# Attention and mixture of experts on one core: x kept as two fp16 halves from the attention on, and x^T made by transposing these halves

## The chip, the cores and the metric

The kernel runs on one core of one Trainium2 chip. The core has five engines that run side by side, each through its own list of instructions in order: PE (TensorE, matrix products and transposes), DVE (VectorE), ACT (ScalarE), POOL (GpSimd) and SP (SyncE, which here only issues transfers). An engine that has to wait for another holds everything behind it in its own list. The metric is the device time of one execution in microseconds (us); for several executions the median is given.

## The reference

All arithmetic is in fp32. Shapes: q, k, v (8, 8, 576, 64), w_gate (512, 8), w1 (8, 512, 1024), w2 (8, 1024, 512).

```python
out_up = repeat(softmax_attention(mean4(q), mean4(k), mean4(v)), 4)   # on 144 positions
out_local = softmax_attention(q, k, v, only where |i - j| < 4)
x = (out_up + out_local) as [4608 tokens, 512]
logits = x @ w_gate
# the 36864 logits from the largest down: a token goes to the expert of its largest
# logit whose capacity of 576 tokens is not used up
for e in range(8):
    out[tokens of e] = maximum(x[tokens of e] @ w1[e], 0) @ w2[e]
```

`softmax_attention` subtracts the row maximum, takes the exponent, divides by the sum and multiplies with v; the scores have the factor 1/8.

## The kernel before

**Halves.** Where an fp32 value enters a product on PE, it is split into two fp16 numbers: hi is the value times a scale, rounded, and lo is what is left. A product of two such values is three fp16 products: hi hi, hi lo, lo hi. ACT makes each hi, DVE each lo (value times scale minus hi).

**Attention (up to about 296 us).** The tokens are worked in 36 units of 128, four and a half to a batch. The order of every engine's instructions is written out: a table `LOC` gives each step of a unit u a lag, and the steps of all units are issued in the order of u + lag, with the loads and the downsampled attention of each batch (queries and keys averaged over four, tiles kdt, qdz, sd, ptd) placed between them. For one unit: `s0`, `s1` (lag 0.33) compute the local scores on PE; DVE takes the maximum (mx, L444) and subtracts it (sw, L445); ACT takes the exponent of sw (L446), which is issued three steps later; `t` (1.3) transposes sw on PE (L454), and ACT copies it to pt (L465); `v0`, `v1` (1.83) multiply with v on PE (L476), and DVE divides by the sum into the tile x (L404 to L407). `up` (1.7) loads the downsampled result of the unit's rows from DRAM through SP (L416), and `add` (4.5, L484) adds it to x, on DVE for the units under 28 and on POOL from there. `st` (4.6, L487) stores x as fp32 to DRAM from SP. `lt` (5.61, L494 to L499) transposes x on PE as four 128x128 fp32 blocks, ACT makes the hi half of x^T out of PSUM and DVE the lo half two steps later; `lm` (8.07, L509 to L514) multiplies these with w_gate into the logits lg. The tile x has 6 buffers, xt 3; all PSUM tiles of the attention are one tile `g` with 8 buffers.

**Routing.** The greedy assignment is a chain of short steps on DVE, PE and ACT (comparisons cmp, counts pR, cs, fl), one pass for each expert. It ends in the list idx of an expert's tokens. The pass for the first expert stands alone (296 to about 334 us); the pass for expert i + 1 runs beside the products of expert i.

**Experts (334 to 787 us).** Here the order comes from a scheduler with priorities. `gather` fetches the 576 rows of x for an expert in five blocks (four of 128 tokens, one of 64) by indirect transfers from POOL into xg (L1061, 5 buffers). They become x^T, tile xt, in one of two ways. For expert 0, `piece` transposes the four fp32 128x128 parts of a block on PE into a PSUM tile pX (L1070), and ACT and DVE split them (L1073, L1074). For experts 1 to 7, `piece_dma` splits the rows first, on ACT and DVE into the tile xs (L1080, L1081, 2 buffers), and SP then issues a transfer that transposes both halves (L1082). `mlp` multiplies with w1 into pH (L1097), ACT and DVE split relu(pH) into ht (L1110, L1113), and the second product goes tile by tile into pX (L1126): tiles c0 to c3 of 128 tokens and c4 of 64. ACT scales a tile into y (L1131), and POOL scatters it to the output (L1134). pX has 2 buffers. The table `GET` places the transposing of expert i + 1: its blocks 0 and 1 after tile c0 of expert i, blocks 2 and 3 after c1, block 4 after c2. The weights are loaded as nat and split into wh and wl (L1044, L1046).

Of the kernel before, what the change touches and what calls it, by code (L numbers as in the profile page):

```python
# [43 lines left out]
FL = 3  # L44
FT = 2
# [4 lines left out]
LOC = {'up': 1.7, 'st': 4.6, 't': 1.3, 'lm': 8.07, 's0': 0.33, 's1': 0.331, 'lt': 5.61, 'v0': 1.83, 'v1': 1.831, 'add': 4.5}  # L50
GS1 = ''
# [4 lines left out]
UB = 3  # L56
XB = 6
NPT = 2
# [18 lines left out]
EN0 = 24  # L77
TB = 3
SUM0 = (0.55, 1.4, 1.89)
# [10 lines left out]
class Attention:  # L90
    def __init__(self, ctx, tc, q, k, v, wg, ident, identb, maskc, x_dram, up_dram, lg, big, more=()):
# [13 lines left out]
        self.load_nat(0, "t")  # L105
        self.ident, ident = ident
        identh = cst.tile([128, 130 + H], BF, name="identb")
# [25 lines left out]
    def gate(self):  # L133
        nc = self.nc
        nc.scalar.activation(self.wg16[:, :, 0], self.wgf, AF.Copy, scale=GS)
        nc.vector.scalar_tensor_tensor(self.wg16[:, :, 1], self.wgf, GS, self.wg16[:, :, 0],
                                       op0=OP.mult, op1=OP.subtract)
# [343 lines left out]
    def log_a(self, u):  # L481
        nc = self.nc
        x = self.x[u]
        (nc.gpsimd if u >= ADDU else nc.vector).tensor_tensor(x, x, self.up[u], op=OP.add)  # L484

    def store(self, u):
        getattr(self.nc, STQ).dma_start(self.x_dram[128 * u:128 * u + 128], self.x[u])  # L487

    def log_t(self, u):
        nc = self.nc  # L490
        x = self.x[u]
        p = self.ps.tile([128, 4, 128], F32, name="g", bufs=8)
        for c in range(4):
            nc.tensor.transpose(p[:, c], x[:, 128 * c:128 * c + 128], self.ident)  # L494
        xt = self.wk.tile([128, 2, 4, 128], F16, name="xt", bufs=TB)
        pf = p.rearrange("p c t -> p (c t)")
        hi = xt[:, 0].rearrange("p c t -> p (c t)")
        nc.scalar.activation(hi, pf, AF.Copy, scale=XS)
        self.after(FT, lambda: nc.vector.scalar_tensor_tensor(xt[:, 1].rearrange("p c t -> p (c t)"), pf, XS, hi,  # L499
                                                              op0=OP.mult, op1=OP.subtract), ("x", u))  # L500
        self.xt[u] = xt

    def log_m(self, u):
        nc = self.nc
        self.need(("x", u))
# [32 lines left out]
    def run(self, after, ready):  # L538
        self.so, self.x, self.up, self.xt, self.ptd = {}, {}, {}, {}, {}
        self.warm()  # L540
# [12 lines left out]
        for b in range(B):  # L553
# [28 lines left out]
            "st": lambda u: lambda: self.store(u),  # L582
            "add": lambda u: lambda: self.log_a(u),
            "lt": lambda u: lambda: self.log_t(u),
            "lm": lambda u: lambda: self.log_m(u),
# [33 lines left out]

W1S, W2S, XM = 64.0, 64.0, 8.0  # L620
LOP = 512
# [3 lines left out]
HALF = {16: ((0, NT),), 32: ((0, 20), (20, NT)), 64: ((0, 20), (20, NT)), 128: ((0, 12), (12, 24), (24, NT))}  # L625
XSB = 2
LOE = "vector"
RACT = True
# [16 lines left out]
class Routing:  # L645
# [37 lines left out]
    def open(self, ctx, ps, ident):  # L683
# [6 lines left out]
        self.t128 = wk.tile([128, NT, 18], BF, name="t128")  # L690
        self.id16 = wk.tile([128, 128], F16, name="id16")
        nc.scalar.copy(self.id16, ident)
        nc.scalar.dma_start(self.tri, consts["tri"])
# [307 lines left out]
class Experts:  # L1001
# [50 lines left out]
    def gather(self, idx, first):  # L1052
# [5 lines left out]
        for c, (s0, n) in enumerate(SL):  # L1058
            xg = self.wk.tile([128, HD], F32, name="xg", bufs=5)
            with self.tc.high_priority():  # L1060
                self.fetched = nc.gpsimd.indirect_dma_start(out=xg[:n], out_offset=None, in_=self.x,  # L1061
                                                            in_offset=bass.IndirectOffsetOnAxis(
                                                                ap=idx[:n, c:c + 1], axis=0))
            xgs.append(xg)

        def piece(c):
            s0, n = SL[c]
            p = self.ps.tile([128, 4, 128], F32, name="pX", bufs=2)
            for d in range(4):
                nc.tensor.transpose(p[:, d, :n], xgs[c][:n, 128 * d:128 * d + 128], self.ident[:n, :n])  # L1070
            hi, lo = xt[:, 0, :, s0:s0 + n], xt[:, 1, :, s0:s0 + n]
            with self.tc.high_priority():
                nc.scalar.activation(hi, p[:, :, :n], AF.Copy, scale=XM)  # L1073
                nc.vector.scalar_tensor_tensor(lo, p[:, :, :n], XM, hi, op0=OP.mult, op1=OP.subtract)  # L1074

        def piece_dma(c):
            s0, n = SL[c]
            xs = self.wk.tile([128, 2, HD], F16, name="xs", bufs=XSB)
            with self.tc.high_priority():
                nc.scalar.activation(xs[:n, 0], xgs[c][:n], AF.Copy, scale=XM)  # L1080
                getattr(nc, LOE).scalar_tensor_tensor(xs[:n, 1], xgs[c][:n], XM, xs[:n, 0], op0=OP.mult, op1=OP.subtract)  # L1081
                nc.sync.dma_start_transpose(xt[:, :, :, s0:s0 + n].rearrange("p a d s -> p (a d) s"),  # L1082
                                            xs[:n].rearrange("p a d -> p (a d)"))

# [64 lines left out]
def moe_attention(tc, q, k, v, wg, w1, w2, cst, out):  # L1149
    nc = tc.nc  # L1150
    with ExitStack() as top:
        dr = top.enter_context(tc.tile_pool(name="dr", bufs=1, space=DRAM))
        keep = top.enter_context(tc.tile_pool(name="keep", bufs=1))
        x_dram = dr.tile([NTOK, HD], F32, name="x_dram")
        up_dram = dr.tile([B * G, HD], F32, name="up_dram")
        lg = keep.tile([128, NT, E], F32, name="lg")
        ident = keep.tile([128, 128], F32, name="ident")
        ro = Routing(top, tc, lg, cst)
        big = top.enter_context(tc.tile_pool(name="big", bufs=6))
        with ExitStack() as ctx:  # L1160
            with tc.manual_schedule(engines=ORD):
                at = Attention(ctx, tc, q, k, v, wg, (ident, cst["ident"]), cst["identb"], cst["mask"], x_dram, up_dram,
                               lg, big, ((ro.tabs, cst["tabs"]),))
                at.run(lambda a, b: ro.setup(a, b, True), ro.ready)
        with ExitStack() as ctx:
            ps = ctx.enter_context(tc.tile_pool(name="mps", bufs=1, space=PSUM))
            ro.open(ctx, ps, ident)
            ex = Experts(ctx, tc, x_dram, w1, w2, out, ident, ps, big)
            with tc.high_priority(TOP):
# [98 lines left out]
```

## Time and profile before

| | us |
|---|---|
| three runs, median | 799.38 |
| lowest and highest of them | 798.59, 804.76 |
| the profiled execution | 796.83 |
| its span in the profile | 795.0 |
| busy in the span: PE, DVE, ACT, POOL | 684.7, 562.3, 333.4, 235.1 |

The granted clock of TensorE was 0.928 of full speed on the mean. A line of a group reads: source line, engine, operation, output <- input (partitions x elements, type), count | busy us, mean ns of one | us for which the engine sat idle just before such an instruction, and what it waited for. A line of the timeline reads: start us, us, engine, line, operation, tiles, count, and in brackets the idle time before it with what ended it; an entry with xN holds N instructions. SPq is the queue of transfers that SP issues. A line of waits reads: waiter <- what ended the wait: us in all, times, longest.

### The profile page before, as it was taken

To read this page: it belongs to the slowest core of one execution; us is meant where nothing else is said; L and a number is where in the kernel's file an instruction comes from. 1 tells how busy PE (TensorE), PEld (TensorE's weight loads), DVE (VectorE), ACT (ScalarE), POOL (GpSimd) and SP (SyncE) were. 2 spreads that over 40 slices of the span, in tenths; PEclk is the share of its full clock that TensorE was granted. 3 is DMA by queue.
4 is the path that set the end of the run, shared out by engine and by line. 5 is a ranking of instruction groups with operands and counts; after the bars stand their busy time and mean duration, and the time that the engine had idled before them with its cause. 6 is when DMAs were issued, how large, how long until landed. Compare 5 with 4: busy or idle time off the path is not lost.

```text
span 795.0 us, 21152 instructions
## 1 busy us (share of the span) xinstructions
PE 684.7 (86%) x8545; PEld 472.8 (59%) x8545; DVE 562.3 (71%) x1679; ACT 333.4 (42%) x631; POOL 235.1 (30%) x274
## 2 busy tenths in 40 slices
PE   6687988796988873499889899999999979999994
PEld 4576877685877752365456356456456456574752
DVE  6878877977797887887869889888869335172210
ACT  3456756573767440342525234234324134252210
POOL 9264463735355440300400412130220311301001
PEclk8789998998999995599989999999999999999997
DMA  9949979697999850611825744480946832704001
GB/s 265 210 129 238 244 195 268 183 255 204 254 228 211 201 173 9 207 66 59 274 60 212 139 151 162 85 307 2 245 147 233 177 113 94 166 1 100 21 28 34
DMA packets 152901, 126.18 MB, mean 159 GB/s; under 512 B 96996, under 2 KB 127204, under 8 KB 152804
## 3 DMA queue, kind: packets, MB, share of 16 engines
q1 hardware_dynamic: 145424, 103.30, 49.9%
q0 software_dynamic: 6432, 20.98, 8.7%
q8 instruction: 68, 1.11, 0.6%
q10 hardware_dynamic: 948, 0.55, 0.3%
q14 instruction: 29, 0.24, 0.1%
HBM read 95.30 MB, written 21.23 MB: 147 GB/s over the span
## 4 chain that ended last, share of the span: by engine, by line
issue 30%; PE 25%; DVE 20%; DMA 13%; ACT 5%; POOL 4%; SPq 2%; POOLq 0%; ACTq 0%; DVEq 0%
PE pH L1097 7%; PE pX L1126 3%; DMA xt<-xs 3%; POOL out_dram L1134 3%; DMA nat<-in_v_dram 2%; DVE cmp L700 2%; PE g L476 2%; PE g L436 2%; PE g L292 2%; DMA xg<-x_dram,idx 2%; PE pR L726 1%; DMA up_dram<-xu 1%; DVE x L407 1%; PE g L454 1%; PE g L325 1%
## 5 line engine op out<-in xcount | busy, mean ns | idle before, releaser
L1097 PE MATMUL pH<-xt,wh 128*128 128x256 f16 (+1 forms) x1024 | 200.1, 291 | 5.7 <-DMA xt<-xs 5.0
L1126 PE MATMUL pX<-wh,ht 128*128 128x512 f16 (+1 forms) x640 | 183.3, 384 | 0.2 <-ACT y L1131 0.2
L1097 PE MATMUL pH<-xt,wl 128*128 128x320 f16 (+1 forms) x512 | 148.5, 290 | 0.0
L1126 PEld LDWEIGHTS <-ht 128*128 128x128 f16 (+1 forms) x960 | 81.5, 101 | 89.2 <-issue 6.4
L1134 POOL DMA_INDIRECT out_dram<-y,idx x40 | 41.2, 1031 | 289.5 <-ACT y L1131 262.9
L1126 PE MATMUL pX<-wl,ht 128*128 128x512 f16 (+1 forms) x320 | 119.3, 384 | 0.0
L1097 PEld LDWEIGHTS <-wh 128*128 128x128 f16 x1024 | 98.2, 99 | 33.2 <-issue 9.1
L1110 ACT ACTIVATE ht<-pH 128x512 f16<-128x512 f32 (+1 forms) x128 | 45.5, 407 | 128.3 <-PE pH L1097 128.3
L1046 DVE SCALAR_TENSOR_TENSOR wl<-nat,wh 128x512 f16<-128x512 f32 x128 | 85.2, 682 | 2.5
L1113 DVE SCALAR_TENSOR_TENSOR ht<-pH,ht 128x512 f16<-128x512 f32 (+1 forms) x128 | 52.4, 450 | 38.7 <-ACT ht L1110 38.3
L1061 POOL DMA_INDIRECT xg<-x_dram,idx x40 | 43.3, 1083 | 118.2 <-DVE idx L997 57.1
L1131 ACT ACTIVATE y<-pX 128x512 f32<-128x512 f32 (+1 forms) x40 | 23.6, 593 | 117.7 <-PE pX L1126 76.4
L1044 ACT ACTIVATE wh<-nat 128x1024 f16<-128x1024 f32 x64 | 66.8, 1055 | 6.6 <-DMA nat<-in_moe_w_dram 6.5
L1081 DVE SCALAR_TENSOR_TENSOR xs<-xg,xs 128x512 f16<-128x512 f32 (+1 forms) x35 | 23.5, 687 | 50.3 <-ACT xs L1080 50.1
L1097 PEld LDWEIGHTS <-wl 128*128 128x128 f16 x512 | 50.6, 99 | 13.0 <-issue 0.4
L465 ACT COPY pt<-g 64x512 f32<-64x512 f32 x72 | 41.8, 580 | 34.2 <-PE g L454 33.0
L292 PE MATMUL g<-ident,nat 128*128 128x128 f32 x256 | 41.7, 292 | 13.7 <-DMA nat<-in_q_dram 9.5
L476 PE MATMUL g<-vw,pt 128*64 128x65 f32 x1152 | 44.5, 230 | 2.4 <-DMA up_dram<-xu 1.4
L476 PEld LDWEIGHTS g<-vw,pt 128*64 128x64 f32 x1152 | 39.5, 143 | 8.4 <-ACT pt L465 4.5
L278 ACT COPY kt<-g 64x512 f32<-64x512 f32 (+1 forms) x56 | 35.1, 627 | 20.7 <-PE g L292 13.8
L278 ACT COPY qz<-g 64x512 f32<-64x512 f32 (+1 forms) x52 | 33.0, 634 | 21.4 <-PE g L292 19.1
L265 POOL TENSOR_TENSOR gtmp<-qz 64x576 f32<-64x576 f32 x28 | 32.5, 1160 | 30.7 <-DVE kdt L268 29.1
(219 smaller groups left out, 1180.1 us busy)
## 6 DMA issues: line engine op xcount, KB each, us to landing
nat<-in_moe_w_dram SPq DMA_DIRECT2D x28, 1024.0 KB
vw<-in_v_dram SPq DMA_DIRECT2D x136, 96.0 KB
up<-up_dram SPq DMA_DIRECT2D x36, 256.0 KB
x_dram<-x SPq DMA_DIRECT2D x36, 256.0 KB
nat<-in_q_dram SPq DMA_DIRECT2D x16, 512.0 KB
nat<-in_k_dram SPq DMA_DIRECT2D x16, 512.0 KB
nat<-in_v_dram SPq DMA_DIRECT2D x14, 512.0 KB
up_dram<-xu SPq DMA_DIRECT2D x16, 128.0 KB
```

Source lines behind the costliest of these rows:

```text
L278: self.nc.scalar.copy(out, in_)
L292: nc.tensor.transpose(p[:, a, :, fp], src[:, 4 * hh + 2 * a + s, 2 * fp:2 * fp + 2].rearrange("p f d -> p (f d)"), self.ident)
L465: self.nc.scalar.copy(out, in_)
L476: nc.tensor.matmul(o[64 * i:64 * i + 64, 65 * h:65 * h + 65], pt[:, 2 * g + i, h].rearrange("p b q -> p (b q)"), self.vw[u % 4][:, i, 4 * ...
L1044: nc.scalar.activation(hi, r, AF.Copy, scale=sc)
L1046: nc.vector.scalar_tensor_tensor(lo[:, a:a + LOP], r[:, a:a + LOP], sc, hi[:, a:a + LOP], op0=OP.mult, op1=OP.subtract)
L1061: self.fetched = nc.gpsimd.indirect_dma_start(out=xg[:n], out_offset=None, in_=self.x, in_offset=bass.IndirectOffsetOnAxis(ap=idx[:n, c:c ...
L1097: mm = nc.tensor.matmul(p[:, s, :s1 - s0], w[d][a][:, 128 * f:128 * f + 128], xt[:, b, d, s0:s1], start=j == 0, stop=j == len(seq) - 1)
L1110: last = nc.scalar.activation(hi, q, AF.Relu)
L1113: nc.vector.scalar_tensor_tensor(lo, q, 0.0, hi, op0=OP.max, op1=OP.subtract)
L1126: nc.tensor.matmul(p[o:o + m], ht[:, f, h0:h0 + m], w[4 + f // 2][b][:, 512 * (f % 2):512 * (f % 2) + 512], start=j < parts, stop=j >= len ...
L1134: i = nc.gpsimd.indirect_dma_start(out=self.out, in_=y[:n], in_offset=None, out_offset=bass.IndirectOffsetOnAxis(ap=idx[:n, c:c + 1], axis=0))
```

## The change

x leaves the attention as two fp16 halves. Two new steps follow the add: `hi` (lag 4.6) makes 32 x rounded to fp16 on ACT, out of the SBUF tile x, and `lo` (4.85) the rest on DVE; both go into a new tile xh with 2 buffers. `st` (now 4.9) stores xh, so that a row of x in DRAM is 1024 fp16 numbers in place of 512 fp32 ones. `lt` transposes the halves as eight fp16 blocks into one PSUM tile, and ACT copies all 1024 columns at once; the DVE step behind it is gone, and `lm` comes a unit earlier (7.07). `gather` fetches the halves. Experts 0 and 1 (`ROWS = 2`) now have their blocks transposed on PE, eight fp16 parts each, with a copy on ACT and one on DVE; experts 2 to 7 have them transposed by the transfer straight out of xg, and the tile xs with its two operations is gone. x's scale XM goes from 8 to 32, xg from 5 to 7 buffers, x from 6 to 4, xt of the attention from 3 to 2, and the fp16 identity is made during the attention.

```diff
-LOC = {'up': 1.7, 'st': 4.6, 't': 1.3, 'lm': 8.07, ..., 'lt': 5.61, 'v0': 1.83, 'v1': 1.831, 'add': 4.5}
+LOC = {'up': 1.7, 'hi': 4.6, 'lo': 4.85, 'st': 4.9, 't': 1.3, 'lm': 7.07, ..., 'lt': 5.61, 'v0': 1.83, 'v1': 1.831, 'add': 4.5}
-XB = 6
+XB = 4
+XHB = 2
-TB = 3
+TB = 2
+    def high(self, u):
+        nc = self.nc
+        self.xh[u] = self.wk.tile([128, 2, HD], F16, name="xh", bufs=XHB)
+        nc.scalar.activation(self.xh[u][:, 0], self.x[u], AF.Copy, scale=XS)
+
+    def low(self, u):
+        nc = self.nc
+        xh = self.xh[u]
+        nc.vector.scalar_tensor_tensor(xh[:, 1], self.x.pop(u), XS, xh[:, 0], op0=OP.mult, op1=OP.subtract)
+
     def store(self, u):
-        getattr(self.nc, STQ).dma_start(self.x_dram[128 * u:128 * u + 128], self.x[u])
+        getattr(self.nc, STQ).dma_start(self.x_dram[128 * u:128 * u + 128], self.xh[u].rearrange("p a d -> p (a d)"))
     def log_t(self, u):
-        p = self.ps.tile([128, 4, 128], F32, name="g", bufs=8)
-        for c in range(4):
-            nc.tensor.transpose(p[:, c], x[:, 128 * c:128 * c + 128], self.ident)
+        p = self.ps.tile([128, 2, 4, 128], F16, name="g", bufs=8)
+        for a in range(2):
+            for c in range(4):
+                nc.tensor.transpose(p[:, a, c], xh[:, a, 128 * c:128 * c + 128], self.id16)
         xt = self.wk.tile([128, 2, 4, 128], F16, name="xt", bufs=TB)
-        nc.scalar.activation(hi, pf, AF.Copy, scale=XS)
-        self.after(FT, lambda: nc.vector.scalar_tensor_tensor(xt[:, 1]..., pf, XS, hi, op0=OP.mult, op1=OP.subtract), ("x", u))
+        nc.scalar.copy(xt.rearrange("p a c t -> p (a c t)"), p.rearrange("p a c t -> p (a c t)"))
...
-W1S, W2S, XM = 64.0, 64.0, 8.0
+W1S, W2S, XM = 64.0, 64.0, XS
+ROWS = 2
-            xg = self.wk.tile([128, HD], F32, name="xg", bufs=5)
+            xg = self.wk.tile([128, 2, HD], F16, name="xg", bufs=7)
         def piece(c):
-            p = self.ps.tile([128, 4, 128], F32, name="pX", bufs=2)
-            for d in range(4):
-                nc.tensor.transpose(p[:, d, :n], xgs[c][:n, 128 * d:128 * d + 128], self.ident[:n, :n])
+            p = self.ps.tile([128, 2, 4, 128], F16, name="pX", bufs=2)
+            for a in range(2):
+                for d in range(4):
+                    nc.tensor.transpose(p[:, a, d, :n], xgs[c][:n, a, 128 * d:128 * d + 128], self.ident[:n, :n])
-                nc.scalar.activation(hi, p[:, :, :n], AF.Copy, scale=XM)
-                nc.vector.scalar_tensor_tensor(lo, p[:, :, :n], XM, hi, op0=OP.mult, op1=OP.subtract)
+                nc.scalar.copy(xt[:, 0, :, s0:s0 + n], p[:, 0, :, :n])
+                nc.vector.tensor_copy(xt[:, 1, :, s0:s0 + n], p[:, 1, :, :n])
         def piece_dma(c):
-            xs = self.wk.tile([128, 2, HD], F16, name="xs", bufs=XSB)
-                nc.scalar.activation(xs[:n, 0], xgs[c][:n], AF.Copy, scale=XM)
-                getattr(nc, LOE).scalar_tensor_tensor(xs[:n, 1], xgs[c][:n], XM, xs[:n, 0], op0=OP.mult, op1=OP.subtract)
                 nc.sync.dma_start_transpose(xt[:, :, :, s0:s0 + n].rearrange("p a d s -> p (a d) s"),
-                                            xs[:n].rearrange("p a d -> p (a d)"))
+                                            xgs[c][:n].rearrange("p a d -> p (a d)"))
-        x_dram = dr.tile([NTOK, HD], F32, name="x_dram")
+        x_dram = dr.tile([NTOK, 2 * HD], F16, name="x_dram")
-                    xt2, piece2 = ex.gather(idx2, False)
+                    xt2, piece2 = ex.gather(idx2, i + 1 < ROWS)
```

Each of the following listings has one instruction to a line: source line, operation, output <- input, and the shape of a tile. The first place is ACT late in the attention, where the exponents (ACTIVATE sw<-sw), the copies of transposed scores (pt) and the work for x^T (xt, and now xh) follow each other. Before:

```order
L446 ACTIVATE sw_131<-sw_131 128x8x38
L465 COPY pt_133<-g 64x16x32 x2
L446 ACTIVATE sw_132<-sw_132 128x8x38
L498 ACTIVATE xt<-g 128x512
L465 COPY pt_134<-g 64x16x32 x2
L498 ACTIVATE xt<-g 128x512
L446 ACTIVATE sw_131<-sw_131 128x8x38
```

and with the change:

```order
L466 COPY pt_135<-g 64x16x32 x2
L491 ACTIVATE xh<-x 128x512
L509 COPY xt<-g 128x1024
L447 ACTIVATE sw_132<-sw_132 128x8x38
L466 COPY pt_134<-g 64x16x32 x2
L447 ACTIVATE sw_133<-sw_133 128x8x38
L491 ACTIVATE xh<-x 128x512
L509 COPY xt<-g 128x1024
L466 COPY pt_135<-g 64x16x32 x2
```

The hi half of a unit stands ahead of the copy for the unit before it, and in the first of these rows both stand ahead of an exponent. On DVE the subtraction sw, whose exponent that is, comes just before the add that the hi half reads:

```order
L496 SCALAR_TENSOR_TENSOR xh<-x,xh 128x512
L522 TENSOR_REDUCE lg<-g 128x8
L445 TENSOR_REDUCE mx<-g 128x8
L446 TENSOR_TENSOR sw_132<-g,mx 128x8x38
L485 TENSOR_TENSOR x<-x,up 128x512
L405 TENSOR_SCALAR den<-g 128x4
```

The lo half (first row) stands where the lo half of x^T stood; the rest of DVE's rows here is as before.

The second place is PE between the tiles c0 and c1 of expert 0's second product. Before, with pX_6504 as c0 and pX_6550 as c1:

```order
L1126 MATMUL pX_6504<-wl7_6384,ht_6251 128x512
L1126 LDWEIGHTS ht_6251
L1126 MATMUL pX_6504<-wh7_6383,ht_6251 128x512
L771 LDWEIGHTS f_5890
L771 MATMUL pR_6171<-one_73,f_5890 72x1
L774 LDWEIGHTS tri_5475
L774 MATMUL pR_6173<-f_5890,tri_5475 128x72
L1126 LDWEIGHTS ht_6251
L1126 MATMUL pX_6550<-wh4_6281,ht_6251 128x512
```

With the change, where pX_6779 is block 1 of expert 1 (block 0 stands some rows above it) and pX_6800 is c1:

```order
L744 LDWEIGHTS id16_64
L744 MATMUL pR_7090<-cs_7088,id16_64 32x8
L1081 LDWEIGHTS xg_6479
L1081 MATMUL pX_6779<-id16_64,xg_6479 128x128
L1133 LDWEIGHTS ht_6487
L1133 MATMUL pX_6800<-wh4_6517,ht_6487 128x512
L749 LDWEIGHTS one_74
L749 MATMUL pR_7097<-fl_7095,one_74 128x8
```

The transposes of expert 1's blocks 0 and 1, and with them the routing steps for expert 1 and 2 that were spread over c1 to c3, now stand ahead of c1.

The third place is SP, the stores and the loads of a stretch of the attention. Before:

```order
L487 DMA x_dram<-x 128x512
L416 DMA up<-up_dram 128x1x512
L229 DMA vw_130<-in_v_dram 48x8x64 x4
L487 DMA x_dram<-x 128x512
L416 DMA up<-up_dram 128x1x512
L229 DMA vw_127<-in_v_dram 48x8x64 x4
```

and with the change:

```order
L417 DMA up<-up_dram 128x1x512
L499 DMA x_dram<-xh 128x1024
L230 DMA vw_131<-in_v_dram 48x8x64 x4
L417 DMA up<-up_dram 128x1x512
L499 DMA x_dram<-xh 128x1024
L230 DMA vw_128<-in_v_dram 48x8x64 x4
```

The store has moved behind the load of up.

More of the change, by code (lines that the diff above doesn't have):

```diff
@@ L49 @@
 DWS = {0: (1.96, 3.4), 7: (0.82, 2.25)}
-LOC = {'up': 1.7, 'st': 4.6, 't': 1.3, 'lm': 8.07, 's0': 0.33, 's1': 0.331, 'lt': 5.61, 'v0': 1.83, 'v1': 1.831, 'add': 4.5}
+LOC = {'up': 1.7, 'hi': 4.6, 'lo': 4.85, 'st': 4.9, 't': 1.3, 'lm': 7.07, 's0': 0.33, 's1': 0.331, 'lt': 5.61, 'v0': 1.83, 'v1': 1.831, 'add': 4.5}
 GS1 = ''
@@ L105, in __init__ @@
         self.load_nat(0, "t")
-        self.ident, ident = ident
+        self.ident, ident, self.id16 = ident
         identh = cst.tile([128, 130 + H], BF, name="identb")
@@ L134, in gate @@
         nc = self.nc
+        nc.scalar.copy(self.id16, self.ident)
         nc.scalar.activation(self.wg16[:, :, 0], self.wgf, AF.Copy, scale=GS)
@@ L583, in run @@
             "add": lambda u: lambda: self.log_a(u),
+            "hi": lambda u: lambda: self.high(u),
+            "lo": lambda u: lambda: self.low(u),
             "lt": lambda u: lambda: self.log_t(u),
@@ L690, in open @@
         self.t128 = wk.tile([128, NT, 18], BF, name="t128")
-        self.id16 = wk.tile([128, 128], F16, name="id16")
-        nc.scalar.copy(self.id16, ident)
+        self.id16 = ident
         nc.scalar.dma_start(self.tri, consts["tri"])
@@ L1157, in moe_attention @@
         ident = keep.tile([128, 128], F32, name="ident")
+        id16 = keep.tile([128, 128], F16, name="id16")
         ro = Routing(top, tc, lg, cst)
@@ L1161, in moe_attention @@
             with tc.manual_schedule(engines=ORD):
-                at = Attention(ctx, tc, q, k, v, wg, (ident, cst["ident"]), cst["identb"], cst["mask"], x_dram, up_dram,
+                at = Attention(ctx, tc, q, k, v, wg, (ident, cst["ident"], id16), cst["identb"], cst["mask"], x_dram, up_dram,
                                lg, big, ((ro.tabs, cst["tabs"]),))
@@ L1166, in moe_attention @@
             ps = ctx.enter_context(tc.tile_pool(name="mps", bufs=1, space=PSUM))
-            ro.open(ctx, ps, ident)
-            ex = Experts(ctx, tc, x_dram, w1, w2, out, ident, ps, big)
+            ro.open(ctx, ps, id16)
+            ex = Experts(ctx, tc, x_dram, w1, w2, out, id16, ps, big)
             with tc.high_priority(TOP):
```

16 lines of the change are left out of this document (4 added, 12 removed).

## The prediction

> **What bounds the kernel now.** I read the page's 40 slices first, then the windows, the groups, and last the timeline at the places that the change touches.
>
> ```profile
> span 795.0 us, 21152 instructions
> PE   6687988796988873499889899999999979999994
> PEclk8789998998999995599989999999999999999997
> ```
>
> Each slice is 19.9 us. Up to slice 14 (the attention, to 296 us) PE stands at 6 to 9 tenths; then comes the bare routing (3, 4, clock 5); from slice 17 PE is the bound wherever it is at 9. So time is gained or lost in the attention, and in the expert slices where PE falls below 9.
>
> ```profile
> 200.00:208.00 8.00, 7.69 (x162) 6.37 (x161) 6.05 (x15) 7.75 (x18) 0.00 (x0) 1.00 1.08 268
> sum 240.00, PE 203.69 PEld 175.09 DVE 197.07 ACT 148.22 POOL 113.86; mean PE 25.46 PEld 21.89 DVE 24.63 ACT 18.53 POOL 14.23
> 372.90:390.00 17.10, 16.18 (x111) 7.50 (x112) 16.67 (x58) 9.00 (x13) 6.07 (x5) 1.00 0.81 295
> 390.00:410.00 20.00, 14.92 (x113) 7.62 (x112) 12.97 (x37) 6.12 (x9) 6.06 (x6) 0.78 0.59 137
> 430.00:460.00 30.00, 25.11 (x195) 12.55 (x193) 25.38 (x76) 13.32 (x20) 9.32 (x8) 1.00 0.67 166
> 560.00:580.00 20.00, 18.26 (x129) 8.10 (x127) 16.49 (x56) 5.65 (x12) 7.59 (x8) 1.00 1.04 291
> 630.00:650.00 20.00, 15.24 (x97) 9.25 (x96) 4.88 (x8) 5.32 (x10) 5.74 (x6) 0.91 0.53 125
> ```
>
> The columns are PE, weight loads, DVE, ACT and POOL busy, then clock, DMA share and GB/s; the sum is over 56 to 296 us, eight windows of 30 us. There PE idles 240 - 203.7 = 36.3 us, DVE 42.9, and ACT is free for 91.8, but not in every stretch: 7.75 of 8 us at 200. Among the experts PE idles 4.9 us at 430 to 460, 1.7 at 560 and 4.8 at 630, 11.4 in all.
>
> **The change part by part.** First the prices, from the grouped rows (before's line numbers):
>
> ```profile
> L498 ACT ACTIVATE xt<-g 128x512 f16<-128x512 f32 x36 | 21.5, 597 | 10.4 <-PE g L494 9.8
> L1080 ACT ACTIVATE xs<-xg 128x512 f16<-128x512 f32 x28 | 16.9, 625 | 20.5 <-DMA xg<-x_dram,idx 11.2 <-DMA xt<-xs 8.9 <-DMA out_dram<-y,idx 0.5
> L1044 ACT ACTIVATE wh<-nat 128x1024 f16<-128x1024 f32 x60 | 62.5, 1055 | 4.2 <-DMA nat<-in_moe_w_dram 4.1
> L499 DVE SCALAR_TENSOR_TENSOR xt<-g,xt 128x512 f16<-128x512 f32 x36 | 24.5, 682 | 1.4 <-ACT xt L498 1.1
> L1081 DVE SCALAR_TENSOR_TENSOR xs<-xg,xs 128x512 f16<-128x512 f32 x28 | 18.8, 689 | 37.5 <-ACT xs L1080 37.4
> L484 DVE TENSOR_TENSOR x<-x,up 128x512 f32<-128x512 f32 x28 | 30.0, 1073 | 7.4 <-DMA up<-up_dram 7.4
> L494 PE MATMUL g<-ident,x 128*128 128x128 f32 x144 | 24.4, 294 | 1.1 <-POOL x L484 0.9 <-issue 0.2
> 290.29 0.63 PE L494 MATMUL g<-ident,x 128*128 128x128 f32 x4
> ```
>
> *Work per unit.* On ACT the 0.597 of L498 goes; the hi half from SBUF costs 0.625 (as L1080, same shape and source) and the 128x1024 copy 1.055 (as L1044; twice L498 is the upper bound, 1.19). So +1.08 a unit, 39 us over 36. DVE's lo half is 0.689 for 0.682: nothing. The stored bytes are the same 2 KB a token. PE gets eight fp16 transposes for four fp32 ones; the four take 0.63 together, and with half the bytes in each I take no change. At the four's own pace per transpose they would cost 0.6 more a unit, at half of it per byte 0.3 less; PE has idle time on both sides of them.
>
> *Where the new ACT work stands (A).* This is the largest term. In 15 of the 36 units the new order on ACT is hi, copy, exponent, where it was copy, exponent. The hi half reads x after the add. So the exponent, whose input is older, now waits for the add and for 1.68 us of other work. One such unit before:
>
> ```profile
> 256.23 0.60 ACT L498 ACTIVATE xt<-g 128x512 f16<-128x512 f32 x1 [0.49 <-PE g L494]
> 257.31 0.46 ACT L446 ACTIVATE sw<-sw 128x304 f32<-128x304 f32 x1 [0.48 <-DVE sw L445]
> 256.30 0.46 DVE L444 TENSOR_REDUCE mx<-g 128x8 f32<-128x304 f32 x1
> 257.19 1.71 DVE L484 TENSOR_TENSOR x<-x,up 128x512 f32<-128x512 f32 x1
> 257.82 0.65 PE L454 MATMUL g<-ident,sw 128*128 128x128 f32 x4 [0.26 <-ACT sw L446]
> ```
>
> The add ends at 258.90; hi to 259.53, copy to 260.58, exponent to 261.04: the transposes L454, and everything behind them on PE, would start 3.2 us later than 257.82. With an add of the mean 1.07 us it is 2.6. But DVE, which was the later engine here, catches up about 1 us while PE waits, so 1.5 is the lower end. I take 2.2. The cover is PE's wait for this exponent, and it is already short:
>
> ```profile
> PE g L454 <- ACT sw L446: 10.3, 10, 2.4
> 113.77 0.66 PE L454 MATMUL g<-ident,sw 128*128 128x128 f32 x4 [1.84 <-ACT sw L446]
> 183.95 0.66 PE L454 MATMUL g<-ident,sw 128*128 128x128 f32 x4 [1.18 <-ACT sw L446]
> 122.73 1.08 PE L292 MATMUL g<-ident,nat 128*128 128x128 f32 x4 [3.19 <-DMA nat<-in_q_dram]
> 194.06 1.09 PE L292 MATMUL g<-ident,nat 128*128 128x128 f32 x4 [5.76 <-DMA nat<-in_q_dram]
> 155.97 0.46 ACT L446 ACTIVATE sw<-sw 128x304 f32<-128x304 f32 x1 [1.44 <-DVE sw L445]
> 158.80 0.87 PE L454 MATMUL g<-ident,sw 128*128 128x128 f32 x4
> ```
>
> Eight of the 15 are exponents whose transposes follow at once; the other seven are like the one at 155.97, which PE needs only at 158.80, 2.4 us after its end: hidden. Of the eight, those at 113 and 183 are followed by a wait for a q load (3.19 and 5.76 us), and that load hangs on SP and DMA, not on PE, so it swallows them. Six times 2.2 is 13 us; the rest of the 39 us of ACT work lies in ACT's idle time, but for about 1 us in stretches as full as that at 200. A = +14 (0 to +30). The store moves past the `up` load on SP and waits for the lo half; what is queued behind it is the next loads of v, or of q and k at a batch's end, which run ahead: 0. At the end of the attention the last unit gets 1.1 us longer, mostly under DVE's comparisons for the routing: +0.5.
>
> *Expert 0's own pieces.* ACT's work halves, DVE copies for a subtraction, PE transposes equal: 0.
>
> *Expert 0 to expert 1 (D).* Expert 1's blocks are now transposed on PE, through the two PSUM buffers of expert 0's second product, and between its tile c0 and its tile c1. So c1 waits until expert 1's rows are routed, gathered and transposed:
>
> ```profile
> 372.92 0.60 ACT L1131 ACTIVATE y<-pX 128x512 f32<-128x512 f32 x1 [5.00 <-PE pX L1126]
> 384.74 0.66 DVE L997 TENSOR_TENSOR idx<-sm 32x5 int32<-32x5 f32 x4
> 386.19 1.48 POOL L1061 DMA_INDIRECT xg<-x_dram,idx  x1 [3.19 <-PE pX L1126]
> 391.08 1.27 ACT L1080 ACTIVATE xs<-xg 128x512 f16<-128x512 f32 x2 [2.42 <-DMA xg<-x_dram,idx]
> 372.90:392.00 19.10, 2.83 (x51) 1.66 (x9) 1.00 0.79 283
> ```
>
> c0 is done at 372.9. The indices end at 385.4, the first block has landed at 391.0 (ACT takes it at 391.08), the second follows; with 0.66 of transposes c1 starts at about 392. In those 19.1 us PE has the routing's 2.83 us (last row: the pR tiles alone), so it idles 16.3. Before, it idled 0.9 up to 390 and 5.1 up to 410, where it waited for the same blocks: 6.0 in all, which the gap replaces. That is +10.3; the 40 transposes add five times 0.66, 3.3. Off go 2 us for the low clock of 390 to 410 (0.78), part of which the new gap's own end repeats, and about 0.5 because the routing meets an empty PE. D = +11 (+5 if the routing hurries, +14 if the low clock comes on top).
>
> *Experts 2 to 7 (E).* No split stands between gather and DMA transpose, and DVE does not wait in it:
>
> ```profile
> 399.53 0.69 DVE L1081 SCALAR_TENSOR_TENSOR xs<-xg,xs 128x512 f16<-128x512 f32 x1 [1.62 <-ACT xs L1080]
> 453.65 0.16 PE L740 MATMUL pR<-fl,one 32*128 32x8 bf16 x1 [2.31 <-DVE fl L738]
> 643.23 0.43 PE L1097 MATMUL pH<-xt,wh 128*128 128x320 f16 x2 [4.60 <-DMA xt<-xs]
> 620.74 19.91 SPq L1082 DMA_TRANSPOSE xt<-xs  x5
> ```
>
> The second row is a routing step late on DVE, the third the transposes being late; both are what the split's hand-overs delay (the fourth row's five transposes are spread over 19.9 us, each waiting for its block). Of the 11.4 us of idle PE, and some 1.7 us of low clock at 630 (0.91 of 20), I take 10 back (-4 if the transfers are slow by themselves, -13 if all goes). Where PE is full, the ACT and DVE time saved is worth nothing.
>
> **Sum**: 14 + 0.5 + 0 + 11 - 10 = +15.5. The profiled execution took 796.8 (span 795.0 and 1.8 around it), so 812.3 there. It ran 2.6 us below the median 799.4; on the median, 815.
>
> The Trainium skill, "TensorE: Matmul & The Clock Gate", section "Part 4: PE-mode transpose", puts one 128x128 bf16 transpose at about 275 ns in a kernel's context. By that as a pitch, the eight of a unit would be an estimated 2.2 us and 36 units some 55 us more. The trace has 294 ns for one, but 0.63 us for four: the time is a latency that overlaps.
>
> **The rivals.**
> 1. The attention hides the late exponents, because a batch's pace is set by loads and DVE elsewhere. For it speaks the wait of 5.76 at 194, against it that only two such waits are seen. A = +1: 802.
> 2. It is faster: PSUM is freed after one copy and no DVE step (A = -2), the routing hurries (D = +5), all late stalls go (E = -13): 790. The one mechanism is the hand-over between ACT and DVE, which L1081's 37.4 us of waiting shows; it decides once the delay of an exponent is below its slack. Against it stands that PE already waits at ten of them.
> 3. The seven hidden exponents are not hidden, since POOL's port or the fuller ACT eats their 2.4 us: thirteen times 2.2 and 1, A = +30: 831.
> 4. The late stalls stay, the DMA transposes being slow (19.9 us for five): E = -4: 821.
> 5. The transposes don't overlap: 8 x 0.294 - 0.63 = 1.7 us a unit, 62 us, less 36.3 of idle PE: 841.
>
> **How the numbers follow.** My forecast 0.45, the rivals in turn 0.21, 0.12, 0.11, 0.08, 0.03. One per cent, about what a measurement here can tell from no change, is 791.4 and 807.4. Faster is rival 2: 0.12. Same is rival 1 and the forecast's lower edge (0.03): 0.24. Slower is the rest: 0.64. The range 798 to 830 leaves out rival 2, half of rival 3 and rival 5, 0.20. The forecast's own is 806 to 824.
>
> **What would show it.** A: the transposes L454 wait longer for the exponent, 20 us or more in the attention for 10.3, and its end moves from 296 to about 310. D: a hole of some 16 us on PE after expert 0's first y, clock 0.5 behind it. E: PE at 9 tenths or more from expert 2 to the end. If the attention ends by 300, A was wrong; if the hole is under 10 us, D.

## The result, and the profile after

The change makes the kernel slower: 834.90 us median of four runs (831.35 to 837.89) against 801.38 (798.59 to 804.76), a ratio of 1.044 with a 95% interval of 1.039 to 1.049. The forecast was 815, with a range to 830; the direction was right and the size too small by some 20 us. Here and below, medians are of all executions, and ratios leave out those that fell in a slower state. The profiled execution has a span of 832.9 us, 37.9 more than before.

The page after, the busy tenths in 40 slices (now of 20.8 us each):

```profile
span 832.9 us, 21570 instructions
PE   7686688867878778429949999999999999999994
PEclk9698798988789898558959999999999999999998
```

The bare routing, the 4 and 2 in PE's row, stands one slice further to the right, and the slices are longer: some 45 us later. Behind it PE has a single 4 and then only nines up to the last slice, where before the row had 8 and 7 up to slice 32. So the loss lies ahead of the routing and a gain behind it. Windows over the attention (from 56 us to the load of the routing's table `tri` that stands at its end), before and after, show PE, weight loads, DVE, ACT, POOL busy, clock, DMA share and GB/s:

```profile
56.00:296.00 240.00, 203.69 (x4585) 175.09 (x4582) 197.07 (x522) 148.22 (x290) 113.86 (x144) 0.94 0.89 222
```

```profile
56.00:340.70 284.70, 217.94 (x4659) 186.97 (x4657) 199.49 (x518) 181.16 (x324) 117.49 (x146) 0.86 0.75 187
```

The attention takes 44.7 us longer. PE is idle for 66.8 us in place of 36.3, which is 30.5 of it; the other 14.2 are PE being busy for longer, at a clock of 0.86 instead of 0.94. That this is the clock and not the new transposes shows in a run below (all new steps later), which has the same instructions in the attention in another order and keeps PE busy for 202.8 us, at 0.94. What PE and ACT wait for, from the waits after:

```profile
PE g L455 <- ACT sw L447: 41.3, 13, 6.3
ACT xh L491 <- DVE x L485: 21.5, 7, 4.9
ACT xh L491 <- DMA x_dram<-xh: 19.8, 7, 7.3
PE g L356 <- ACT sd L340: 10.0, 11, 2.5
ACT xh L491 <- DVE den L405: 8.4, 5, 4.0
```

PE's wait for the exponent (transposes of sw, L455) has gone from 10.3 to 41.3 us. ACT itself waits in front of the hi half: for the add, as forecast, and, which no term of the forecast had, for the store of an earlier unit to let go of one of the two xh buffers. One such place in the timeline after:

```profile
87.74 0.68 DVE L496 SCALAR_TENSOR_TENSOR xh<-x,xh 128x512 f16<-128x512 f32 x1
90.26 0.39 SPq L216 DMA_DIRECT2D nat<-in_k_dram  x1
90.93 0.34 SPq L499 DMA_DIRECT2D x_dram<-xh  x1
96.44 0.63 ACT L491 ACTIVATE xh<-x 128x512 f16<-128x512 f32 x1 [7.35 <-DMA x_dram<-xh]
97.10 0.69 DVE L496 SCALAR_TENSOR_TENSOR xh<-x,xh 128x512 f16<-128x512 f32 x1 [5.30 <-ACT xh L491]
98.00 0.46 ACT L447 ACTIVATE sw<-sw 128x304 f32<-128x304 f32 x1
98.52 1.11 PE L455 MATMUL g<-ident,sw 128*128 128x128 f32 x4 [6.29 <-ACT sw L447]
```

The halves are complete at 88.4. SP issues their store at 90.9, since it first issues the loads that stand ahead of it, and ACT goes on at 96.4, when the trace has the store as landed. ACT has waited for the buffer for 7.35 us by then; with it waited DVE (for the hi half), the exponent, and PE (for the exponent). The four transposes then take 1.11 us where 0.60 to 0.66 is usual: after some 6 us with hardly any work on PE the granted clock is 0.50 (98.5 to 99.7 us). So a gap is paid twice. The Trainium skill, "TensorE: Matmul & The Clock Gate", section "Why this matters for your kernels", warns of gaps over some 3 us between bursts for this reason; the trace agrees with 1.11 against 0.60 to 0.66.

In the experts, from the end of c0 of expert 0, before (to 410 us, and a long stretch behind it) and after (to the start of c1, and a long stretch):

```profile
372.90:410.00 37.10, 31.10 (x222) 15.12 (x223) 29.64 (x95) 15.12 (x22) 12.13 (x10) 0.88 0.69 210
410.00:650.00 240.00, 225.24 (x1823) 133.73 (x1822) 187.49 (x661) 83.68 (x156) 47.28 (x45) 0.99 0.55 161
```

```profile
417.90:434.70 16.80, 5.87 (x82) 4.96 (x83) 13.97 (x46) 4.12 (x8) 6.10 (x6) 0.57 0.81 284
460.00:690.00 230.00, 226.24 (x1834) 135.84 (x1831) 170.16 (x590) 73.20 (x136) 52.28 (x51) 1.00 0.57 171
```

The hole behind c0 is there: c1 starts at 434.7, and until then PE is idle for 10.9 of 16.8 us, at a clock of 0.57. In the long stretch PE idles 3.8 us of 230, where it was 14.8 of 240.

### The profile page after: what moved, and what is told of

It reads as the page before. It is cut to its first block, busy times and chain, and to the rows that moved or that the text cites. A ratio compares the mean times of both kernels' runs of the same rounds, so it can differ in the third digit from the quotient of the medians.

```text
span 832.9 us, 21570 instructions
## 1 busy us (share of the span) xinstructions
PE 696.5 (84%) x8749; PEld 486.4 (58%) x8749; DVE 547.3 (66%) x1649; ACT 350.1 (42%) x637; POOL 235.8 (28%) x274
## 4 chain that ended last, share of the span: by engine, by line
PE 34%; DVE 22%; issue 21%; DMA 9%; ACT 8%; POOL 3%; SPq 1%; ACTq 0%; POOLq 0%; DVEq 0%
PE pH L1104 11%; PE pX L1133 7%; DMA x_dram<-xh 4%; POOL out_dram L1141 2%; ACT xt L509 2%; DVE cmp L709 2%; PE g L437 2%; PE g L455 2%; PE g L293 2%; PE pR L735 2%; PE g L477 1%; ACT xh L491 1%; DVE wl L1055 1%; DVE x L485 1%; DVE xh L496 1%
## 5 line engine op out<-in xcount | busy, mean ns | idle before, releaser
L1104 PE MATMUL pH<-xt,wh 128*128 128x256 f16 (+1 forms) x1024 | 194.5, 287 | 1.0 <-ACT xt L1083 0.7
L1104 PE MATMUL pH<-xt,wl 128*128 128x320 f16 (+1 forms) x512 | 146.7, 287 | 0.0
L455 PE MATMUL g<-ident,sw 128*128 128x128 f32 x144 | 27.8, 326 | 44.2 <-ACT sw L447 44.2
L1140 DVE SCALAR_TENSOR_TENSOR y<-pX,y 64x512 f32<-64x512 f32 x8 | 5.5, 693 | 89.7 <-ACT y L1138 89.6
L477 PE MATMUL g<-vw,pt 128*64 128x65 f32 x1152 | 46.5, 237 | 3.2 <-ACT pt L466 3.2
L491 ACT ACTIVATE xh<-x 128x512 f16<-128x512 f32 x36 | 22.6, 629 | 59.5 <-DVE x L485 21.5
L477 PEld LDWEIGHTS g<-vw,pt 128*64 128x64 f32 x1152 | 41.6, 150 | 8.2 <-ACT pt L466 4.2
L455 PEld LDWEIGHTS g<-ident,sw 128*128 128x128 f32 x144 | 19.4, 165 | 46.2 <-ACT sw L447 43.0
```

The costliest lines, as they stand in the source:

```text
L455: nc.tensor.transpose(p[:, 128 * i:128 * i + 128], t[:, 2 * i:2 * i + 2].rearrange("p h k -> p (h k)"), self.ident)
L477: nc.tensor.matmul(o[64 * i:64 * i + 64, 65 * h:65 * h + 65], pt[:, 2 * g + i, h].rearrange("p b q -> p (b q)"), self.vw[u % 4][:, i, 4 * ...
L1104: mm = nc.tensor.matmul(p[:, s, :s1 - s0], w[d][a][:, 128 * f:128 * f + 128], xt[:, b, d, s0:s1], start=j == 0, stop=j == len(seq) - 1)
```

## The experiments

Every ratio is that of the runs of a kernel to runs of the kernel before on the same chip, with its 95% interval. The executions of the kernel before that count in the ratios had medians of 799.3 to 806.1 on these chips, so between chips the ratios are to be compared and not the times. Theory O held that the order on ACT made the loss (the hi half and the copy ahead of the exponent), theory B that the two xh buffers did.

**Exponent first.**

```diff
-FL = 3
+FL = 1
```

> The changed kernel with FL 1 for 3: the exponent of a unit is issued right behind its subtraction, so it stands ahead of the hi half and the copy on ACT. Theory O (the order on ACT is the cost): PE's wait for the exponent falls from 44 us to about its 10 to 16 of before, and the time from 835 to about 808 (the 42 us that the attention grew, less the 15 or so that the hi half's own waits for its buffer leave). Theory B (the two xh buffers, held by the store, are the cost): ACT still stops at the hi half, everything behind it waits as before, and the time stays within 825 to 835.

845.55 us, ratio 1.0486 (1.0432 to 1.0541): no gain in the whole time, and above what either theory allowed. Both theories' signs are in the waits, which for this and the next two kernels are taken from 56 to 300 us; here exponent first:

```profile
ACT xh L491 <- DMA x_dram<-xh: 20.6, 6, 5.9
PE g L356 <- ACT sd L340: 20.2, 11, 5.0
PE g L455 <- ACT sw L447: 9.7, 5, 2.6
```

PE's wait for the exponent did fall to 9.7, as theory O has it. But ACT still stands for 20.6 us at the hi half, and PE now waits for what comes next behind it on ACT, the exponents of the downsampled attention (sd). Much of the wait has only changed its name.

**Three buffers.** The tile that warms PE up takes the fp16 identity's place, which makes the room.

```diff
-XHB = 2
+XHB = 3
-        self.wm = cst.tile([128, 128], BF, name="wm")
+        self.wm = self.id16
```

> The changed kernel with three xh buffers for two (the tile for warming PE up shares the fp16 identity's place, for room). Theory B: ACT's wait for the store in front of the hi half, 19.8 us, is gone, and with it about as much of the time: 815 to 820. Theory O: the order still makes the exponent wait for the add, the hi half and the copy; the time falls by less than 8, to 827 or more.

831.78 us, ratio 1.0316 (1.0274 to 1.0358): about 10 us better than the change by the ratios, less than theory B expected. The wait for the store is gone, and ACT waits for the add in its place, 38.5 us in 18 times, with PE still waiting behind it:

```profile
ACT xh L491 <- DVE x L485: 38.5, 18, 4.9
PE g L455 <- ACT sw L447: 27.8, 8, 5.0
```

**Both.**

> Both at once: exponent first and three xh buffers. If the two causes are separate costs, the gains of the two runs add, and the attention ends near 296 to 300 us again: 793 to 800, since the experts' part of the changed kernel is some 7 us shorter than before. If they are one chain (ACT stops at the hi half, and the exponent is behind it), either of them alone brings nearly all, and this run is within 4 us of the better one.

817.39 us, ratio 1.0112 (1.0057 to 1.0167), worse than the 793 to 800 of separate costs and much better than either edit alone. In the whole time the two together bring 0.033, or 26 us, and singly 0 and 10. These figures hold a disturbance: from c0 to the end the three kernels took 429 to 432 us, the change 415, with the same program there (see "The change again"). So the attention by itself, up to the load of `tri`, is the cleaner measure. In order, the run with ROWS 1 (the next one, on the same chip, with the attention of the change), exponent first, three buffers, and both:

```profile
56.00:341.50 285.50, 218.23 (x4659) 187.63 (x4658) 199.38 (x519) 180.92 (x324) 117.67 (x146) 0.86 0.74 187
56.00:336.00 280.00, 221.22 (x4737) 189.60 (x4736) 202.59 (x523) 183.58 (x326) 118.47 (x145) 0.88 0.76 190
56.00:327.90 271.90, 213.50 (x4662) 183.31 (x4662) 198.92 (x520) 181.58 (x325) 118.25 (x147) 0.88 0.79 196
56.00:311.40 255.40, 212.16 (x4734) 182.14 (x4731) 202.58 (x523) 183.23 (x326) 119.14 (x145) 0.90 0.83 209
```

Singly they take 5.5 and 13.6 us off the attention, together 30.1. Each is one trace, and executions with the same attention ended up to 6 us apart, so the 5.5 alone may be nothing; that the two together bring more than their sum stays: with the one cause left, the other's wait fills part of the time. Neither was the whole, and some 15 us of the attention were still missing. The waits of this kernel show where PE and ACT still wait:

```profile
PE g L356 <- ACT sd L340: 12.0, 11, 2.5
ACT xh L491 <- DVE x L485: 10.5, 15, 1.2
PE g L455 <- ACT sw L447: 9.6, 4, 2.6
PE g L507 <- DVE xh L496: 9.0, 13, 1.4
```

The last row is PE waiting at the transposes of the halves for the lo half.

**ROWS 1 in the change.**

```diff
-ROWS = 2
+ROWS = 1
```

> The changed kernel with ROWS 1: expert 1's blocks go by DMA transposes too, and nothing of them stands in pX between c0 and c1 of expert 0. Theory of the prediction (D costs 11): the hole of some 11 us on PE behind expert 0's c0 is gone and the time falls by 8 to 12, to about 825. Rival (the hole only takes the place of the stalls that were at the same place before): the time falls by 0 to 5, or PE waits for the DMA transposes at the start of expert 1 instead.

835.69 us, ratio 1.037 (1.0327 to 1.0413), for 1.041 to 1.044 of the change: 3 to 6 us, inside the intervals, and nearer to the rival. The trace agrees: from c0 to the end 414.7 us, for 415.0 of the change. But the change itself did not run on this chip, where the three kernels with ROWS 2 needed 15 us more there, so the comparison is not a firm one.

**The two parts apart.** For these, the gathers read a constant table, so that either half of the change runs with the other half of the kernel before.

```diff
-            ex = Experts(ctx, tc, x_dram, w1, w2, out, ident, ps, big)
+            ex = Experts(ctx, tc, cst["rows"], w1, w2, out, ro.id16, ps, big)
```

> The attention of before with the experts of the change. So that the halves exist without the attention making them, the gathers fetch their rows from a constant table of fp16 numbers of the same row size in place of x's rows; the output is then not the reference's. From the traces (first tile of expert 0 to the end: 415 us with the change, 422 before) the experts' part gains 7 us: ratio 0.99. Theory of the prediction (D +11, E -10): no gain, ratio 1.00.

790.61 us, ratio 0.9885 (0.9823 to 0.9947). The experts' part is a gain of 9 us; from c0 to the end the trace has 415.7 us, for 422.1 before.

> As the run before, with ROWS 1: expert 1 by DMA transposes. If the hole behind expert 0's c0 costs what the prediction gave it (11 us), this is 11 us faster than the run before; if it only takes the place of stalls, within 4 us of it.

781.91 us, ratio 0.9765 (0.9693 to 0.9836); one of its four executions took 2199.57 us, and the others lie close to the median. Without the hole the experts gain 18.8 us, 9.6 more than with it (the intervals overlap a little), and take 405.2 us from c0 on. That is the gain with the constant table; the whole kernels with ROWS 1 in this document took 408 to 416 us there, four of six within 2 us of the change's 415. PE in the same stretches as above, now 3.4 us idle in the first and 4.9 in the long one:

```profile
375.10:412.10 37.00, 33.64 (x278) 17.98 (x277) 28.57 (x92) 13.06 (x21) 15.34 (x10) 0.95 0.67 195
412.10:652.10 240.00, 235.09 (x1902) 142.60 (x1901) 184.81 (x643) 80.38 (x149) 54.03 (x50) 1.00 0.61 180
```

> The attention of the change with the experts of before: the gathers fetch fp32 rows from a constant table, and the experts split them as before; the output is not the reference's. If the whole loss is made in the attention, its end stands near 340 us and the ratio is 1.05, above the 1.044 of the whole change. If the loss came from the experts, it is under 1.03.

836.16 us, ratio 1.0473 (1.0396 to 1.055): the attention's part is a loss of 38 us. The two parts, 1.0473 and 0.9885, give 1.036 together, within the interval of the change on the same chip, which follows.

**The change again.**

> The change itself once more, as the measure for the runs on this chip: ratio 1.044 as before, and in its trace no other waits than in the first. If its experts take 430 us here, as in three of the runs before, and not 415, then part of what those runs showed was the chip and not the edit.

833.61 us, ratio 1.0412 (1.0331 to 1.0493), and a trace like the first one. From c0's end its experts take 415 us again, while in the first three runs, with the same instructions in the same order there, they took 429 to 432 on another chip. So the profiles of those three runs are read above for the attention alone.

**Towards a better one.** The combination, without the hole:

```diff
-FL = 3
+FL = 1
-XHB = 2
+XHB = 3
-ROWS = 2
+ROWS = 1
```

> Exponent first, three xh buffers and ROWS 1 together. If the parts add: the exponent and buffer run stood at 1.011, and ROWS 1 took 0.012 off the experts alone: 0.999, no change against before. If the gains share a cause, 1.005 to 1.011.

805.80 us, ratio 1.0036 (0.999 to 1.0082): no change against before, and 0.0076 better than with ROWS 2 on the other chip, with overlapping intervals. Then the transposes of the halves later:

```diff
-'lt': 5.61
+'lt': 5.9
```

> As the run before, and the transposes of the halves at lag 5.9 instead of 5.61, so that they stand behind the products with v on PE. Theory (what is left of the attention's loss is PE waiting at these transposes for the lo half, 12 us over 16 times in the run with exponent first and three buffers): the wait goes, the time falls by 6 to 12 us, ratio about 0.99. Rival (that wait covers others): under 3 us.

799.93 us, ratio 0.9908 (0.9856 to 0.9959): 10 us better by the ratios, 6 by the medians of the two kernels on the same chip, and a little under the time before. What PE waits for in the attention, without and with the later transposes:

```profile
PE g L507 <- DVE xh L496: 12.2, 17, 1.4
PE g L477 <- ACT pt L466: 2.5, 5, 0.8
```

```profile
PE g L477 <- ACT pt L466: 20.2, 15, 2.5
PE g L507 <- DVE xh L496: 1.7, 2, 0.8
```

The wait for the lo half is gone, but one for the copies of the transposed scores (pt) has come in its place, and the attention of the two traces ends at 305.8 and 307.4 us. So the traces do not show how the time was gained, nor that the wait for the lo half was a cost of its own. And instead of moving the exponent, all new steps later, with three buffers and ROWS 1:

```diff
-'hi': 4.6, 'lo': 4.85, 'st': 4.9, 'lm': 7.07, 'lt': 5.61
+'hi': 4.95, 'lo': 5.15, 'st': 5.2, 'lm': 8.07, 'lt': 6.61
```

> Instead of the exponent being moved, the new steps are: hi at 4.95, lo 5.15, store 5.2, transposes 6.61, logits 8.07, with three xh buffers and ROWS 1, and the exponent issued three steps later as in the change. Theory (the loss is the place of the hi half, in front of work that PE waits for): PE's wait for the exponent is 10 to 15 us, and the ratio 0.98 to 0.99, better than the run with the exponent moved, since the hi half now waits for nothing. Rival (ACT's added 39 us of work are the loss, wherever they stand): 1.00 or more.

800.42 us, ratio 0.9905 (0.9849 to 0.9962). Its attention ends at 303.6 us, where the change's ended at 340.7 and that of the kernel before at 296.0, and it has the clock of before (the window is to be read beside the two at the top):

```profile
56.00:303.60 247.60, 202.83 (x4728) 175.15 (x4726) 202.39 (x521) 182.79 (x326) 117.82 (x144) 0.94 0.83 215
```

> The lags of the run before and the exponent first as well. If the place of the hi half was the cause, moving the exponent adds nothing: within 3 us of the run before. If the exponent still waits there for the copy of x^T, it is 5 us faster or more.

798.89 us, ratio 0.9928 (0.9885 to 0.997): the same as the run with the later steps, as the theory has it. With the hi half behind the exponent there is nothing left to gain from moving the exponent.

**Place, load and buffers apart.** The later lags with two buffers:

> As the run with the later lags and ROWS 1, but with two xh buffers as the change has them. Theory (the store holds a buffer whatever the place; two are too few): ACT waits for the store some 15 to 20 us again and the time is 8 to 15 us longer than with three, ratio 1.00 to 1.01. Rival (the buffer wait only shows because the hi half stands so early): within 3 us of three buffers, ratio 0.99.

802.36 us, ratio 1.0027 (0.9988 to 1.0065), against 0.9905 with three: 0.0122, or 10 us, for the buffers by themselves. At the early place the third brought 0.0124 (with the disturbance named above), so the place seems not to matter to it. Then the kernel before with nothing but a hi half that no one reads, at the lags 4.55 and 4.95; for room, x gives up one of its six buffers:

```diff
-XB = 6
+XB = 5
+    def high(self, u):
+        xh = self.wk.tile([128, HD], F16, name="xh", bufs=2)
+        self.nc.scalar.activation(xh, self.x[u], AF.Copy, scale=XS)
```

> The kernel before with one addition: the hi half is made on ACT at lag 4.55, right behind the add, into a tile of two buffers that nothing reads, so that no store or lo half holds it; x has 5 buffers for room, and all else is as before. It adds 36 x 0.63 = 23 us of ACT work in the place of the change, without the wide copy and without a wait for the store. Theory (the place in front of the exponent is the cost): PE's wait for the exponent rises from 10 to 25 us or more, and the time by 10 to 20 us, ratio 1.015 to 1.025. Rival (the cost needs the buffers): ratio within 1.005.

819.91 us, ratio 1.0252 (1.0164 to 1.0341).

> The same addition at lag 4.95, behind the exponent and the products with v. Theory: the same 23 us of ACT work are hidden there, ratio within 1.005, and the difference to the run at 4.55 is the price of the place alone. Rival (ACT's load itself costs): as slow as at 4.55.

805.85 us, ratio 1.0117 (1.0047 to 1.0187). The groups of the hi half and of the transposes behind the exponent, first at 4.55, then at 4.95:

```profile
L488 ACT ACTIVATE xh<-x 128x512 f16<-128x512 f32 x36 | 22.6, 628 | 52.9 <-DVE den L404 26.5 <-DVE x L484 21.5 <-POOL x L484 3.1
L454 PE MATMUL g<-ident,sw 128*128 128x128 f32 x144 | 27.1, 320 | 32.4 <-ACT sw L446 32.4
```

```profile
L488 ACT ACTIVATE xh<-x 128x512 f16<-128x512 f32 x36 | 22.7, 629 | 8.2 <-DVE den L404 7.0 <-DVE lg L518 0.5 <-DVE x L484 0.4
L454 PE MATMUL g<-ident,sw 128*128 128x128 f32 x144 | 24.5, 297 | 12.4 <-ACT sw L446 11.5 <-ACT qz L278 0.9
```

The same 22.6 us of work stand behind 52.9 us of waiting at the one place and 8.2 at the other, and PE's idle time falls from 32.4 to 12.4 with it. The place by itself is 0.0135, or 11 us, by the ratios, 14 by the two medians on the same chip, and the attention ends 12.7 us earlier (304.4 for 317.1). But 0.0117, or 9 us (6 by the medians), stay at the good place too, where the expectation was 0.005 at most. That may be ACT's load, as the rival has it, although ACT is busy for only two thirds of the attention. It may as well be the buffer that x gave up: with the hi half at 4.95 DVE, which writes the division's result into x, waits six times for the store of an earlier unit to let go of a buffer.

```profile
DVE x L407 <- DMA x_dram<-x: 21.0, 6, 7.8
```

The kernel before, with six buffers, has no such wait in the attention, and with the hi half at 4.55 it is 2.6 us. No run has the hi half at 4.95 and six x buffers, so the 9 us are not settled between the two.

## Why the prediction was right in direction and short in size

- **A, the attention: the step that failed, +14 forecast, +38 measured (the attention alone).** The mechanism named first, the exponent behind the hi half, was right, and its size nearly so: "six times 2.2 is 13 us", where the place alone is 11 to 14; that the numbers meet so well is partly luck, since that run has the hi half without the wide copy. What failed is the term that I put at nothing, the store. I wrote that what is queued behind it on SP runs ahead, "0", and looked at who waits behind the store, not at what the store holds: ACT waited 19.8 us for it, and a third xh buffer brings 10 us by the ratios, at the early place and at the late one, of the 24 that A was short. Nor do order and buffers simply add: in the attention alone they bring 5.5 and 13.6 us singly and 30.1 together, and later steps with three buffers bring 37 of the 44.7. What the other 8 us are is open. Here stands also "the rest of the 39 us of ACT work lies in ACT's idle time, but for about 1 us": a hi half alone costs 6 to 9 at the good place, but with one x buffer less, so the runs neither confirm nor refute this step. That the gaps lower PE's clock was left out of A too; it is inside these numbers (14 of the 45 us in the trace).
- **"The other seven are hidden"**: not shown either way. PE's waits for an exponent went from 10 to 13 in the attention, and their mean from 1.0 to 3.2 us, the longest to 6.3. Against such delays a slack of 2.4 us does not hide an exponent, but the list does not tell which exponents these are.
- **The q loads that swallow two waits**: borne out as far as it goes. PE's wait for nat from q, 8.9 us before, is 0.7 after; with the work ahead of it delayed, the load has landed by then.
- **Price of the steps**: hi 0.629 for 0.625, copy 1.011 for 1.055, both right; the lo half was 0.786 on the mean for 0.689, its shortest 0.679 and its longest 1.67.
- **PE's transposes**: eight fp16 ones took 0.61 us in the trace after where nothing held them up, as forecast (0.63 for the four before). Rival 5 is out. The 275 ns of the Trainium skill, "TensorE: Matmul & The Clock Gate", section "Part 4: PE-mode transpose", read as a pitch, would be an estimated 2.2; the trace shows a latency that overlaps, 219 ns for one (the median) and 0.61 us for eight.
- **D, the hole: wrong in size, +11 forecast, about +4 to +5 measured.** PE idles 10.9 us in the hole for the 6.0 that it replaces, 4.9 more, where 16.3 for 6.0 was forecast. From c0 to the end the traces have 422.1 us before and 415.0 after, 7.1 less, and the long stretch's idle time is 14.8 less 3.8 = 11.0 less; so the switch to expert 1 costs about 3.9 net. c1 started 16.8 us after c0, not 19.1, and PE was busy for 5.9 of the hole: the routing's products took 4.4 instead of 2.8, at a clock of 0.57, and the first blocks' transposes, which the forecast counted apart, lie in it too (2.2, partly at the same time). The place itself was as told. Against DMA transposes the hole costs 9.6 with the constant table and 3 to 6 in the whole kernel, where that lies inside the intervals.
- **E, the late stalls: right, -11.0 for -10.** They are gone together with the split, as forecast; that it was the split's hand-overs and not, say, the two more xg buffers was not tested apart. Rival 4, slow DMA transposes, is out.
- **The rivals**: rival 3 (831, none of the delays hidden) came nearest to the time, by luck: it has nothing of the store and its buffers.

What stays open: what the 9 us at the good place are, ACT's load or x's buffer, and with them the last 8 us of the attention. How the later transposes gained 6 to 10 us is open too. Why the experts took some 15 us longer in the three runs with ROWS 2 on one chip is not settled either; the run with ROWS 1 on the same chip did not (414.7 us from c0 on), and it was not tried further.

## What to carry to other kernels

Price a new step on an in-order engine by three things: what it waits for, what stands behind it, and how long its output buffer stays held by the slowest reader, here a store queued behind loads. Two waits on one engine can cover each other, so that removing either alone shows less than its share; change both before a theory is dropped. Watch what an experiment gives up for room: a buffer less can bring in the very wait that is being studied. Where a change has two parts, run each with the other part of the old kernel: here that showed a gain of 1.2% inside a loss of 4.4%, and led to versions at 0.99 of the time before.

## What the runs showed of the hardware that was not expected

The same kernel before has medians from 799.3 to 806.1 us on different chips (of the executions that count in the ratios), so that a difference of just under 1% between two runs means nothing without the kernel before beside each. In the three runs with exponent first or three buffers and ROWS 2, DVE stood still for about 4 us twice in front of the same instruction, and the trace names no engine for it; here with three buffers alone:

```profile
510.57 0.19 DVE L741 TENSOR_SCALAR cs<-pR 128x32 f16<-128x32 f32 x1 [4.15 <-remote]
558.55 0.19 DVE L741 TENSOR_SCALAR cs<-pR 128x32 f16<-128x32 f32 x1 [3.83 <-remote]
```

The change itself, whose experts' program is the same, does not show it in either of its traces. With ROWS 1 it is seen once on the same chip, 1.6 us, and twice on another, 3.6 us in all. Two times 4 us would be half of the 15 us that the experts took longer in those three runs.
